# Splitting the value products of a tiled attention kernel by columns

## The chip, the cores and the metric

The kernel runs on one core of a Trainium2 chip. The metric is the device time of one execution in microseconds (us), as the median of several runs. Durations inside an execution come from one execution that was recorded by the hardware profiler.

TensorE is the engine that multiplies matrices (its rows are named PE in the profile, and PEld for the loading of weights that goes before a product). ScalarE (ACT) computes activations, VectorE (DVE) computes elementwise operations and reductions, GpSimd (POOL) does elementwise work on on-chip memory and issues DMAs, and SyncE (SP) issues DMAs. TensorE writes its results into eight accumulator banks of 128 partitions by 512 float32 columns, called `bank` here.

## What is computed

For x of 2048 tokens by 448, the reference mixes a 16-head attention block and an MLP by a gate for each token:

```python
def reference(A_x, A_wqkv, A_wo, B_x, B_w1, B_b1, B_w2, B_b2, gate_w):
    x = A_x
    g = _sigmoid((x * gate_w).sum(-1, keepdims=True))
    a = _A_ref(x, A_wqkv, A_wo)
    b = _B_ref(x, B_w1, B_b1, B_w2, B_b2)
    return g * a + (1 - g) * b
...
    scores = jnp.einsum("bhqd,bhkd->bhqk", q, k) * (Dh ** -0.5)
    p = _softmax(scores, axis=-1)
    o = jnp.einsum("bhqk,bhkd->bhqd", p, v)
```

`_A_ref` is attention with heads of 28 columns and a projection by wo, `_B_ref` is layer norm, a product by w1, GELU, and a product by w2. All data are float32.

## The kernel before

The kernel has three stages. The first one computes queries, keys, values and the gate (lines 125 to 260). The second one is the MLP (lines 435 to 499). The third one is the attention (lines 611 to 715), and the change lies in it.

The 16 heads are treated as 4 groups of 4 heads, and the 2048 queries as 4 chunks of 512 (`CH`). A group and a chunk together give 16 combinations, and the code numbers them `n`; I call each of them a chunk from here on. For each chunk the keys come in 16 steps of 128 (`NT`). One key tile of one head is a unit, so that there are 64 units to a chunk and 1024 in all. The outer loop takes five units at a time (`U`); such a turn crosses steps and chunks freely, there are 205 turns, and a chunk lasts 12.8 of them.

A turn consists of these parts, in the order in which TensorE gets them:

- `scores` (line 620) makes the score tiles of the first three units in banks 0 to 2. Each tile is the sum of three products of 28 or 29 rows by 512 columns (line 629), since keys and queries are held as a high and a low part. ScalarE then takes the exponential of the three banks in one instruction (line 634) into a tile `pt`. The other two units follow in banks 3 and 4, with a second exponential. Products of different heads use different groups of 32 rows of the array.
- In between up to three tiles of the row maximum of a later chunk are made in banks 5, 6 and 5 (`filler.max.issue`, line 321). VectorE reduces each of them (line 301). `filler.due` deals them out evenly over the turns until the maxima of all chunks are there.
- The value products `pv_mm` (line 655) multiply the exponentials by the values, and sum over the 16 steps of a chunk in bank 7. One step is four products, one for each head, of 128 rows by 512 columns; each writes 32 partitions of the bank, so that the four run beside each other in four groups of 32 columns of the array. The operands are float32, and the profile shows two records for each such product, with a weight load before each.

The order on TensorE is the program's order, as is that of the other engines in this loop (`tc.manual_schedule`). The lines that the change touches are 655 to 659 and 698 to 714: after the scores of a turn, all steps whose units had been made by the end of the turn before are summed, in whole steps, and not beyond the end of a chunk. Since a turn brings 1.25 steps, three turns of four sum one step and the fourth sums two.

When a chunk's sum is complete, `finish` (line 535) begins: VectorE copies bank 7 to `ob` (line 540), and GpSimd starts a DMA that gathers the denominators (line 541). The later parts of `finish` follow a fixed number of turns behind (`STEPS`): a reciprocal (line 543), DMAs that spread it (lines 545 and 547), three operations on GpSimd (lines 553 to 555), and in the last group also the projection by wo (lines 525 to 527). The next chunk's first value product has to wait for the copy. After the last turn the remaining steps are summed and `finish_last` (line 565) projects the last chunk and writes it out. There the sums over the denominators are made with four products of 128 by 128 in float32 (line 578).

The tiles `pt` come from a pool with four buffers for the three-unit form and four for the two-unit form.

Of the kernel before, what the change touches and what calls it, by code (L numbers as in the profile page):

```python
# [15 lines left out]
P = 128  # L16
# [5 lines left out]
NG = 4  # L22
CH = 512
NC = S // CH
NT = S // P
# [7 lines left out]
MG = 6  # L33
FS = 4
LQ = 12
STEPS = (2, 5, 7, 8, 9, 10)


@with_exitstack
def kernel(ctx: ExitStack, tc: tile.TileContext, xt, wqk, wv, wo, xk, w1, b1, w2, b2,  # L40
                          ident_d, sel_d, out):
    nc = tc.nc
# [344 lines left out]
    def load_khi(g):  # L387
        if g == MLP_G:
            khi[g] = khr
        else:  # L390
            khi[g] = aq.tile([P, S], F32R, name=f"khi{g}")
            for j in range(4):
                r = D + (4 * g + j) * DH
                nc.sync.dma_start(khi[g][32 * j:32 * j + DH].bitcast(F32), qk[0, r:r + DH])
        nc.sync.dma_start(khi[g][DH:P:32].bitcast(F32),
                          ones.rearrange("(a b) x -> a (b x)", a=1).partition_broadcast(4).rearrange("a o x -> a (o x)"))
# [3 lines left out]
    def load_klo(g):  # L400
        klo[g] = aq.tile([P, S], F32R, name="klo", bufs=2)
        for j in range(4):
            r = D + (4 * g + j) * DH
            nc.sync.dma_start(klo[g][32 * j:32 * j + DH].bitcast(F32), qk[1, r:r + DH])

    vg = {}

    def load_v(g):
        vg[g] = aq.tile([P, NT, P], F32, name="vg", bufs=2)
        for t in (slice(0, 4), slice(4, NT)):  # L410
            nc.sync.dma_start(vg[g][:, t], vs[t, :, g, :].rearrange("t p d -> p t d"))
# [3 lines left out]
    def load_q(n):  # L415

        g, c = divmod(n, NC)
        qs[n] = aq.tile([P, CH], F32R, name="qh", bufs=3), aq.tile([P, CH], F32R, name="ql", bufs=3)
        for i in range(2):
            for j in range(4):  # L420
                r = (4 * g + j) * DH
                nc.sync.dma_start(qs[n][i][32 * j:32 * j + DH].bitcast(F32), qk[i, r:r + DH, c * CH:(c + 1) * CH])

    def load_qm(n):

        while filler.done < min(65 * NG * NC, 65 * (n + 1) + 9):
            filler.max.issue(5, 1)
        g, c = divmod(n, NC)
        nc.sync.dma_start(qs[n][0][DH:P:32].bitcast(F32), ms[g][:, c * CH:(c + 1) * CH])
# [76 lines left out]
    U, UA = 5, 3  # L506
# [83 lines left out]
    def load_wo(g):  # L590
        worw = ao.tile([P, D], F32, name="ob")
        nc.sync.dma_start(worw, wo[:, g])
        nc.vector.tensor_copy(woh[:, g], worw)
        nc.gpsimd.tensor_sub(wol[:, g], worw, woh[:, g].bitcast(F32))

    def load_acc(c):

        a = aq.tile([P, NT, P], F32, name="vg", bufs=2) if c % 2 == 0 else aq.tile([P, S], F32, name="klo", bufs=2)
        if c % 2 == 0:
            a = a.rearrange("p a b -> p (a b)")  # L600
        acc[c] = a[:, :TPC * D].rearrange("p (t d) -> p t d", d=D)
        nc.sync.dma_start(acc[c], gbs[c * TPC:(c + 1) * TPC].rearrange("t p d -> p t d"))

    def gate_acc(c):
        for i in range(TPC):
            a, tt = acc[c][:, i], c * TPC + i
            nc.gpsimd.tensor_add(a, a, b2b)
            nc.gpsimd.tensor_scalar(a, a, ngate[:, tt:tt + 1], None, op0=OP.mult)
# [6 lines left out]

    filler.spread(nc.gpsimd, NG * NC * 65, ((NG * NC - 2) * NT + LQ - 1) * 4 // U)

    probs = {}

    def scores(units, most):  # L620

        def product(u, i):
            n, k, j = u // 4 // NT, u // 4 % NT, u % 4
            g, (qh, ql) = n // NC, qs[n]
            a, b, r = ((khi[g], qh, DH + 1), (klo[g], qh, DH), (khi[g], ql, DH))[i]
            r = slice(32 * j, 32 * j + r)
            nc.tensor.matmul(bank[:, u % U], a[r, k * P:(k + 1) * P], b[r], start=(i == 0), stop=(i == 2))  # L629

        def exps(units):
            t = ap.tile([P, len(units), CH], F32, name=f"pt{len(units)}")
            b = units[0] % U
            nc.scalar.activation(t, bank[:, b:b + len(units)], AF.Exp, scale=SCALE)  # L634
            for i, u in enumerate(units):
                probs[u] = t[:, i]

        first, last = units[:UA], units[UA:]
        if most > 0:
            filler.max.issue(5, 1, [(first[0] + 3) % 4])  # L640
        for i in range(3):
            for u in first:
                product(u, i)
        exps(first)
        for i in range(3):
            for u in last:
                product(u, i)
            if i == 0 and most > 1:
                filler.max.issue(6, 1, [(first[0] + 1) % 4, (first[0] + 2) % 4])
        if last:  # L650
            exps(last)
        if most > 2:
            filler.max.issue(5, 1, [(first[0] + 1) % 4, (first[0] + 2) % 4])

    def pv_mm(step):
        n, k = divmod(step, NT)
        for j in range(4):
            nc.tensor.matmul(pv[32 * j:32 * j + 32, :], vg[n // NC][:, k, 32 * j:32 * j + 32], probs.pop(4 * step + j),  # L658
                             start=(k == 0), stop=(k == NT - 1), skip_group_check=True)

    pv = bank[:, 7]
    E = mybir.EngineType
    steps = NG * NC * NT
    with tc.manual_schedule(engines={E.SP, E.Pool, E.Activation, E.DVE}):
        fin = None
        summed = 0
        ready = 0
        at = -1
        since = 0
        for u in range(0, 4 * steps, U):  # L670
            units = list(range(u, min(u + U, 4 * steps)))
            while at < units[-1] // 4:
                at += 1
                n, k = divmod(at, NT)
                g, c = divmod(n, NC)
                if n == 0:
                    if k == 0:
                        load_khi(1)
                        nc.sync.dma_start(b2b, b2.partition_broadcast(P))
                    if 2 <= k < 6:  # L680
                        load_wo(k - 2)
                    if k in (8, 10):
                        load_khi(k // 2 - 2)
                if g == NG - 1:
                    if k == 6:
                        load_acc(c)
                    if k == 10:
                        gate_acc(c)
                if k == 2 and n + 1 < NG * NC:
                    load_q(n + 1)  # L690
                if k == LQ and n + 1 < NG * NC:
                    load_qm(n + 1)
                if g + 1 < NG:
                    if c == 1 and k == 4:
                        load_klo(g + 1)
                    if c == 2 and k == 4:
                        load_v(g + 1)
            scores(units, min(3, filler.due()))
            ended = False
            while summed < ready and not ended:  # L700
                pv_mm(summed)
                summed += 1
                ended = summed % NT == 0
            ready = (units[-1] + 1) // 4
            since += 1
            if ended:
                n = summed // NT - 1
                fin, since = finish(n // NC, n % NC, pv), 0
                next(fin)
            elif fin is not None and since in STEPS:  # L710
                next(fin, None)
        while summed < steps:
            pv_mm(summed)
            summed += 1
        finish_last(NC - 1, pv)


# [51 lines left out]
```

## Time and profile before

| | |
|---|---|
| three runs | 1142.76, 1151.25, 1155.83 us; median 1151.25 us |
| the profiled execution | 1146.98 us, of which the span from the first to the last instruction is 1145.2 us |
| granted TensorE clock, mean over the span | 0.991 |
| attention, first turn to the last value products | about 486 to 1131 us of the span |
| TensorE busy between 500 and 1000 us | over 99.8% in each stretch of 100 us |
| ScalarE busy in the same stretches | 79 to 81% |
| VectorE busy in the same stretches | 68 to 69% |

Times of single instructions are read from the timeline, whose rows give the start in us from the beginning of the span, the duration (for a merged row, from the first start to the last end), the engine, the line, the operation, output and input, shapes and the count. In brackets stands how long the engine had been idle before, and what ended the idle time. Rows of TensorE's products overlap, since products are pipelined and their ends are modelled; the distance between starts is what a sequence costs.

### The profile page before, as it was taken

What the parts mean: (1) busy time and instruction counts of PE and PEld (TensorE: products, weight loads), DVE (VectorE), ACT (ScalarE), POOL (GpSimd) and SP (SyncE); (2) the same over time, 40 slices, a digit from 0 to 9 for tenths busy, and PEclk for the clock granted to TensorE, in tenths of its full rate; (3) what the DMA queues carried; (4) which work ended last, traced back from release to release, by engine and by line L of the source; (5) the groups of instructions that cost most, each with busy time, mean ns of one, the idle gap of its engine ahead of it and who ended that gap; (6) DMA issues with size and microseconds to landing.
All of it is one profiled execution on the core that took longest, in us unless ns stands there. A gap on an engine that the chain in (4) does not pass through costs nothing.

```text
span 1145.2 us, 19823 instructions
## 1 busy us (share of the span) xinstructions
PE 1116.6 (98%) x8136; PEld 678.4 (59%) x8136; DVE 731.6 (64%) x1033; ACT 635.9 (56%) x668; POOL 331.0 (29%) x355
## 2 busy tenths in 40 slices
PE   6999989999999999989999999999999999999998
PEld 4778867777767777744444444444444444454556
DVE  3433287888878888666676766676676667646103
ACT  5324551132033032067887878878787887848463
POOL 4043367146044032011123012311222123444250
PEclk9999999999999999989999999999999999999999
DMA  8878643002100014062101211111121003002201
GB/s 269 277 217 303 208 141 88 25 9 68 47 23 18 25 30 114 25 168 72 30 12 36 52 40 40 36 27 39 31 64 36 18 19 91 12 25 68 66 26 49
DMA packets 53519, 84.35 MB, mean 74 GB/s; under 512 B 8676, under 2 KB 28660, under 8 KB 52628
## 3 DMA queue, kind: packets, MB, share of 16 engines
q1 hardware_dynamic: 49236, 76.96, 22.5%
q0 software_dynamic: 4192, 6.12, 2.1%
q8 instruction: 64, 1.05, 0.4%
q14 instruction: 27, 0.22, 0.1%
HBM read 56.40 MB, written 26.49 MB: 72 GB/s over the span
## 4 chain that ended last, share of the span: by engine, by line
PE 89%; DMA 4%; POOL 3%; DVE 2%; issue 1%; ACT 1%; SPq 0%; POOLq 0%; ACTq 0%; DVEq 0%
PE bank L658 22%; PE bank L629 20%; PE bank L321 15%; PE bank L451 10%; PE bank L168 4%; PE bank L466 4%; PE bank L463 4%; PE bank L464 4%; PE bank L184 2%; PE bank L525 1%; DMA bxr<-in_xk 1%; PE bank L526 1%; PE bank L527 1%; DMA xraw<-in_xt 1%; POOL hl L456 1%
## 5 line engine op out<-in xcount | busy, mean ns | idle before, releaser
L634 ACT ACTIVATE pt<-bank 128x1536 f32<-128x1536 f32 (+1 forms) x410 | 484.6, 1234 | 155.9 <-PE bank L629 155.9
L301 DVE TENSOR_REDUCE mx<-bank 128x1 f32<-128x512 f32 x624 | 413.4, 687 | 174.9 <-PE bank L321 161.0
L658 PE MATMUL bank<-pt,vg 128*32 128x512 f32 x2048 | 263.7, 606 | 0.0
L303 DVE TENSOR_REDUCE mx<-bank 128x2 f32<-128x1024 f32 x200 | 235.4, 1219 | 41.1 <-PE bank L321 41.0
L321 PE MATMUL bank<-khi,qd 28*128 28x512 f32 x512 | 241.6, 479 | 0.3 <-DVE mx L301 0.2
L321 PEld LDWEIGHTS bank<-khi,qd 28*128 28x128 f32 x512 | 92.3, 181 | 148.3 <-DVE mx L301 107.0
L629 PE MATMUL bank<-qh,klo 28*128 28x512 f32 x1024 | 179.0, 395 | 0.0
L629 PE MATMUL bank<-qh,khi 29*128 29x512 f32 x768 | 161.8, 484 | 0.3 <-ACT h L469 0.3
L451 PE MATMUL bank<-y,w1f 128*128 128x512 f32 x616 | 153.2, 400 | 0.6 <-ACT h L455 0.6
L451 PEld LDWEIGHTS bank<-y,w1f 128*128 128x128 f32 x616 | 113.8, 190 | 36.1 <-issue 12.5
L629 PE MATMUL bank<-ql,khi 28*128 28x512 f32 x768 | 133.6, 393 | 0.0
L456 POOL TENSOR_TENSOR hl<-h,hh 128x512 fp32r<-128x512 f32 x56 | 72.5, 1295 | 172.0 <-ACT h L455 160.8
L658 PEld LDWEIGHTS bank<-pt,vg 128*32 128x32 f32 x2048 | 45.7, 108 | 84.6 <-issue 83.1
L629 PEld LDWEIGHTS bank<-qh,klo 28*128 28x128 f32 x1024 | 90.2, 186 | 4.2
L321 PE MATMUL bank<-khr,qd 28*128 28x512 f32 x512 | 80.7, 467 | 7.3 <-DVE mx L303 4.2
L541 POOL DMA_DIRECT2D lt<-ob x15 | 10.8, 723 | 265.7 <-DVE ob L540 265.7
L466 PE MATMUL bank<-w2h,hl 128*128 128x448 f32 x224 | 85.1, 380 | 1.9 <-POOL hl L456 1.9
L469 ACT ACTIVATE h<-bank 128x448 f32<-128x448 f32 x16 | 8.7, 543 | 140.4 <-PE bank L466 140.4
L629 PEld LDWEIGHTS bank<-qh,khi 29*128 29x128 f32 x768 | 63.3, 183 | 36.8 <-ACT pt L634 32.1
L463 PE MATMUL bank<-w2h,hh 128*128 128x448 f32 x224 | 84.7, 378 | 0.3 <-ACT hh L454 0.3
L454 ACT ACTIVATE hh<-bank,b1s 128x512 fp32r<-128x512 f32 x56 | 38.4, 685 | 81.9 <-PE bank L451 81.8
L464 PE MATMUL bank<-w2l,hh 128*128 128x448 f32 x224 | 82.3, 368 | 0.0
(100 smaller groups left out, 1237.0 us busy)
## 6 DMA issues: line engine op xcount, KB each, us to landing
qk<-hl SPq DMA_DIRECT2D x28, 512.0 KB
xraw<-in_xt SPq DMA_DIRECT2D x16, 256.0 KB
vs<-vt SPq DMA_DIRECT2D x16, 256.0 KB
r<-in_xt SPq DMA_DIRECT2D x16, 256.0 KB
rc<-rls POOLq DMA_DIRECT2D x60, 64.0 KB, 2.2
bxr<-in_xk SPq DMA_DIRECT2D x8, 448.0 KB
r<-in_w SPq DMA_DIRECT2D x14, 256.0 KB
gbs<-h SPq DMA_DIRECT2D x16, 224.0 KB
```

Of the source, the lines that this page charges most:

```text
L168: nc.tensor.matmul(ps, a, b, start=(i == 0), stop=(i == len(ops) - 1))
L301: nc.vector.reduce_max(self.mx[:, c0:c0 + 1], bank[:, b0], axis=AX)
L303: nc.vector.reduce_max(self.mx[:, c0:c1 + 1:c1 - c0], bank[:, b0:b1 + 1], axis=AX)
L321: nc.tensor.matmul(bank[:, b], self.qds[self.n][r, i * P:(i + 1) * P], khi[self.n // NC][r, k * 512:(k + 1) * 512], start=True, stop=True)
L451: nc.tensor.matmul(ps, a, b, start=(i == 0), stop=(i == len(ops) - 1))
L456: nc.gpsimd.tensor_sub(hl[f], h, hh[f].bitcast(F32))
L463: nc.tensor.matmul(a, hh[f][:, sl], w2h[f], start=(f == 0), stop=False)
L464: nc.tensor.matmul(a, hh[f][:, sl], w2l[f], start=False, stop=False)
L466: nc.tensor.matmul(a, hl[f][:, sl], w2h[f], start=False, stop=(f == NF - 1))
L629: nc.tensor.matmul(bank[:, u % U], a[r, k * P:(k + 1) * P], b[r], start=(i == 0), stop=(i == 2))
L634: nc.scalar.activation(t, bank[:, b:b + len(units)], AF.Exp, scale=SCALE)
L658: nc.tensor.matmul(pv[32 * j:32 * j + 32, :], vg[n // NC][:, k, 32 * j:32 * j + 32], probs.pop(4 * step + j), start=(k == 0), stop=(k == N ...
```

## The change

The value products are no longer issued in whole steps. `pv_mm` gets a number of columns up to which all has to be summed (512 to a step), and cuts a step where that number falls into it. `share` computes this number for a turn: within a chunk it rises linearly with the turn, from 0.6 turns (`LAG`) after the chunk's first turn to the turn in which its last units are summed, rounded down to a multiple of 128 columns, and never beyond the units that were made by the end of the turn before. In the turn with which a chunk ends, all that is left of it is summed.

```diff
+LAG = 0.6
...
-    def pv_mm(step):
-        n, k = divmod(step, NT)
-        for j in range(4):
-            nc.tensor.matmul(pv[32 * j:32 * j + 32, :], vg[n // NC][:, k, 32 * j:32 * j + 32], probs.pop(4 * step + j),
-                             start=(k == 0), stop=(k == NT - 1), skip_group_check=True)
+    def pv_mm(upto):
+
+        nonlocal summed
+        while summed < upto:
+            step, a = divmod(summed, CH)
+            b = min(CH, a + upto - summed)
+            n, k = divmod(step, NT)
+            for j in range(4):
+                nc.tensor.matmul(pv[32 * j:32 * j + 32, a:b], vg[n // NC][:, k, 32 * j:32 * j + 32],
+                                 probs[4 * step + j][:, a:b], start=(k == 0), stop=(k == NT - 1), skip_group_check=True)
+            summed += b - a
+
+    def share(turn):
+
+
+        ready = turn * U // 4
+        n = min(NG * NC - 1, summed // (NT * CH))
+        first, last = (-(-NT * 4 * i // U) for i in (n, n + 1))
+        part = (turn - first - LAG) / (last - first - LAG)
+        return min(ready, steps, (n + 1) * NT) * CH if part >= 1 else min(ready * CH, n * NT * CH + int(NT * CH * part) // P * P)
...
             scores(units, min(3, filler.due()))
-            ended = False
-            while summed < ready and not ended:
-                pv_mm(summed)
-                summed += 1
-                ended = summed % NT == 0
-            ready = (units[-1] + 1) // 4
+            before = summed // (NT * CH)
+            pv_mm(share(u // U))
+            ended = summed // (NT * CH) > before
             since += 1
             if ended:
-                n = summed // NT - 1
+                n = before
...
-        while summed < steps:
-            pv_mm(summed)
-            summed += 1
+        pv_mm(steps * CH)
```

More of the change, by code (lines that the diff above doesn't have):

```diff
@@ L653, in scores @@
             filler.max.issue(5, 1, [(first[0] + 1) % 4, (first[0] + 2) % 4])
-    def pv_mm(step):
-        n, k = divmod(step, NT)
-        for j in range(4):
-            nc.tensor.matmul(pv[32 * j:32 * j + 32, :], vg[n // NC][:, k, 32 * j:32 * j + 32], probs.pop(4 * step + j),
-                             start=(k == 0), stop=(k == NT - 1), skip_group_check=True)
+    def pv_mm(upto):
[14 more added lines that the diff above has]
+        return min(ready, steps, (n + 1) * NT) * CH if part >= 1 else min(ready * CH, n * NT * CH + int(NT * CH * part) // P * P)
     pv = bank[:, 7]
+    summed = 0
     E = mybir.EngineType
@@ L665 @@
         fin = None
-        summed = 0
-        ready = 0
         at = -1
```

## The prediction, made before the changed kernel was run

> **What bounds the kernel now.** I read the engines' busy time first, then the chain that ended last, then the waits, then the timeline of some turns.
>
> ```profile
> PE 1116.6 (98%) x8136; PEld 678.4 (59%) x8136; DVE 731.6 (64%) x1033; ACT 635.9 (56%) x668; POOL 331.0 (29%) x355
> ...
> PE 89%; DMA 4%; POOL 3%; DVE 2%; issue 1%; ACT 1%; SPq 0%; POOLq 0%; ACTq 0%; DVEq 0%
> PE bank L658 22%; PE bank L629 20%; PE bank L321 15%; PE bank L451 10%; PE bank L168 4%; PE bank L466 4%; PE bank L463 4%; PE bank L464 4%; PE bank L184 2%; PE bank L525 1%; DMA bxr<-in_xk 1%; PE bank L526 1%; PE bank L527 1%; DMA xraw<-in_xt 1%; POOL hl L456 1%
> ```
>
> TensorE is on the chain for 89%, and the three lines of an attention turn (value products 658, scores 629, row maxima 321) hold 57% of the span. A busy TensorE may still hide small waits, and evening out the turns could only win if there are such waits. The table of waits has one that fits:
>
> ```profile
> PEld bank L629 <- ACT pt L634: 40.4, 133, 0.8
> ```
>
> In 133 cases a score's weight load waited for an exponential. Whether this costs time shows in two turns that follow each other, the first of them behind one step of value products (8 records), the second behind two (16):
>
> ```profile
> 704.08 1.07 PE L658 MATMUL bank<-pt,vg 128*32 128x512 f32 x8
> ...
> 705.07 0.18 PEld L321 LDWEIGHTS bank<-khi,qd 28*128 28x128 f32 x1 [0.84 <-DVE mx L301]
> ...
> 705.87 0.18 PEld L629 LDWEIGHTS bank<-qh,khr 29*128 29x128 f32 x2 [0.25 <-ACT pt L634]
> ...
> 706.15 2.37 ACT L634 ACTIVATE pt<-bank 128x1536 f32<-128x1536 f32 x2 [0.34 <-PE bank L629]
> ...
> 706.78 0.16 PEld L658 LDWEIGHTS bank<-pt,vg 128*32 128x32 f32 x8 [0.25 <-issue]
> 706.78 1.92 PE L658 MATMUL bank<-pt,vg 128*32 128x512 f32 x16
> ...
> 708.63 0.18 PEld L321 LDWEIGHTS bank<-khi,qd 28*128 28x128 f32 x1 [0.84 <-issue]
> ...
> 709.72 2.37 ACT L634 ACTIVATE pt<-bank 128x1536 f32<-128x1536 f32 x2 [1.20 <-PE bank L629]
> ...
> 710.34 1.06 PE L658 MATMUL bank<-pt,vg 128*32 128x512 f32 x8
> ...
> 711.33 0.18 PEld L321 LDWEIGHTS bank<-khi,qd 28*128 28x128 f32 x1 [0.84 <-DVE mx L301]
> ```
>
> A turn begins with the weight load of line 321 (705.07, 708.63, 711.33). From there to its value products it takes 706.78 - 705.07 = 1.71 us in the turn that waits 0.25 us for ScalarE, and 710.34 - 708.63 = 1.71 us in the turn behind the double portion, where ScalarE had been idle for 1.20 us and nothing waits for it. So the wait lies beside other work: five units on four row groups mean that one group has six products in a row, and these take the 1.71 us. ScalarE is just in time: its two exponentials end at 706.15 + 2.37 = 708.52, that is 3.45 us after the turn's start. Both kinds of turn are bound by TensorE, with 1.71 us of scores each.
>
> **The change part by part.** One step costs from start to start 705.07 - 704.08 = 0.99 us, two steps 708.63 - 706.78 = 1.85 us. So 512 columns stream in 0.86 us, and 0.13 us are fixed for each turn. A turn of 640 columns then takes 1.25 x 0.86 + 0.13 = 1.21 us. Four turns before: 4 x 1.71 + 3 x 0.99 + 1.85 = 11.66 us. Four after: 4 x (1.71 + 1.21) = 11.68 us. The evening out by itself is worth nothing: columns are moved between turns that TensorE bounds alike.
>
> *Pieces.* Working `share` through for all turns gives 402 pieces in place of 256 whole steps: 110 of 512 columns, 88 of 384, 116 of 256, 88 of 128. That is 146 pieces and 292 passes more (a float32 product runs in two passes; each has four records and four weight loads). No value product under 512 columns is in the trace. The nearest rows are the float32 products of 128 columns behind the last turn, and the weight loads of the value products:
>
> ```profile
> 1132.57 1.05 PE L578 MATMUL bank<-ob,sel 128*128 128x128 f32 x8
> ```
> ```profile
> L578 PE MATMUL bank<-ob,sel x8: 270/275/275, 1132.6 to 1133.3; 128*128 128x128 f32 x8
> ```
> ```profile
> L658 PEld LDWEIGHTS bank<-pt,vg x2048: 106/109/153, 494.2 to 1129.7; 128*32 128x32 f32 x187
> ```
> ```profile
> 707.24 0.13 PEld L658 LDWEIGHTS bank<-pt,vg 128*32 128x32 f32 x4 [0.30 <-issue]
> ```
>
> Eight passes of 128 columns start (1.05 - 0.275) / 7 = 0.111 us apart, although each loads new weights. A quarter of a 512-column pass is 0.86 / 2 / 4 = 0.107 us. So a pass costs about 0.004 us beyond its columns: 292 x 0.004 = 1.2 us. From below the bound is nothing, since all columns are still streamed. From above, every extra pass would pay a whole weight load of 0.109 us: 292 x 0.109 = 31.8 us. In between, a set of four loads takes 0.13 us, which is longer than a 128-column pass by 0.023 us: 176 such passes x 0.023 = 4.0 us. I take 1.2 us, because line 578 is the same type and the same width. The Trainium skill, page "TensorEngine Tiling (Array Packing)", section "Instruction Overhead", speaks against short pieces: it gives each matmul some 60 cycles of overhead, at 2.4 GHz about 0.025 us, an estimate by which the pieces would cost 292 x 0.025 = 7.3 us and the whole change 11 us; the row of line 578 does not show such an overhead.
>
> *The first turn of a chunk.* With `LAG`, a chunk's first value products are 256 columns instead of 512, in the turn behind the one that ended a chunk. There the copy of bank 7 comes before the reductions on VectorE:
>
> ```profile
> 723.06 0.18 PEld L321 LDWEIGHTS bank<-khi,qd 28*128 28x128 f32 x1 [0.84 <-DVE mx L301]
> ...
> 723.27 0.69 DVE L540 COPY ob<-bank 128x512 f32<-128x512 f32 x1 [0.37 <-PE bank L658]
> ...
> 723.88 1.96 DVE L301 TENSOR_REDUCE mx<-bank 128x1 f32<-128x512 f32 x3
> ...
> 724.13 2.37 ACT L634 ACTIVATE pt<-bank 128x1536 f32<-128x1536 f32 x2 [0.28 <-PE bank L629]
> ...
> 724.61 0.18 PEld L321 LDWEIGHTS bank<-khi,qd 28*128 28x128 f32 x1 [0.17 <-DVE mx L301]
> ...
> 725.04 1.06 PE L658 MATMUL bank<-pt,vg 128*32 128x512 f32 x8
> ...
> 726.03 0.18 PEld L321 LDWEIGHTS bank<-khi,qd 28*128 28x128 f32 x1 [0.84 <-DVE mx L301]
> ```
>
> VectorE is done with the third reduction at 723.88 + 1.96 = 725.84. The next turn's first product needs the same bank 5 and begins at 726.03; it doesn't wait. With 256 columns it could begin at 725.04 + 0.99 - 0.43 = 725.60, but waits until 725.84 and about 0.04 us more (the load at 724.61 stands 0.04 us behind the first reduction, 723.88 + 0.69): 725.88, a loss of 0.28 us. All of the turn's scores are queued behind this load on TensorE. The 256 columns that were put off cost their 0.43 us later. ScalarE ends at 724.13 + 2.37 = 726.50, before the second group of the next turn wants its banks (725.88 + 0.80, as 705.87 stands to 705.07), so it adds nothing. Of the 15 chunk ends before the last, 14 lie among turns with row maxima: 14 x 0.28 = 3.9 us. Bounds: nothing, if the copy begins earlier; 0.43 us for each, 6.0 us, if VectorE is late by more.
>
> *Turns without row maxima*, about eight behind 1081 us, are the exception in which ScalarE does bind:
>
> ```profile
> 1084.77 0.21 PEld L629 LDWEIGHTS bank<-qh,khi 29*128 29x128 f32 x4 [0.84 <-ACT pt L634]
> ...
> 1086.37 1.07 PE L658 MATMUL bank<-pt,vg 128*32 128x512 f32 x8
> ...
> 1087.37 0.19 PEld L629 LDWEIGHTS bank<-qh,khi 29*128 29x128 f32 x3 [0.84 <-ACT pt L634]
> 1088.27 0.18 PEld L629 LDWEIGHTS bank<-qh,khi 29*128 29x128 f32 x2 [0.37 <-ACT pt L634]
> ...
> 1089.17 1.06 PE L658 MATMUL bank<-pt,vg 128*32 128x512 f32 x8
> ```
>
> Behind two steps the scores take 1086.37 - 1084.77 = 1.60 us, behind one step 1089.17 - 1087.37 = 1.80 us. Evened out, two turns form a loop: exponentials end 3.45 us after a start, 0.05 us later the next turn's second group begins, 0.90 us later (1089.17 - 1088.27) its value products, then 1.21 us: 5.61 / 2 = 2.81 us a turn. Four turns before were 2 x 1.60 + 2 x 1.80 + 3 x 0.99 + 1.85 = 11.62, after 11.24 us: 0.8 us won over eight turns. The first turn of the last chunk has 256 columns there too; the turn behind it then reaches its value products 3.45 + 0.05 + 0.90 = 4.40 us after that start instead of 1.60 + 0.56 + 1.80 = 3.96: 0.4 us back. I count nothing.
>
> *What does not move.* The instructions of ScalarE, VectorE, GpSimd and SyncE stay in the same order, and every chunk ends in the same turn as before, so `finish` and its DMAs keep their turns. The sums lag the units by at most 1.75 steps, under two turns; with four buffers of `pt` no exponential waits for one. The tail behind the last turn gets 768 columns instead of 512, and turn 204 has 256 fewer: nothing.
>
> The sum: 1.2 + 3.9 = +5.1 us. Against the profiled execution (1146.98 us: span 1145.2 and 1.8 around it) that gives 1152.1 us. That execution lies 4.3 us under the median of the three runs, 1151.25 us, by which it would be 1156.4. I forecast 1154 us, between the two.
>
> **The rivals.** *Slower: TensorE isn't supplied with instructions fast enough.*
>
> ```profile
> 700.00:800.00 100.00, 100.00 (x958) 47.30 (x951) 68.81 (x109) 80.86 (x69) 17.61 (x26) 1.00 0.10 26
> ```
>
> TensorE got 958 products (each with its weight load) in 100 us, one in 0.104 us, and the turn of 26 pairs (15 scores, 3 maxima, 8) in 2.70 us and that of 34 in 3.56 us have the same rate. The changed kernel has on average 18 + 402 x 8 / 204 = 33.8 pairs in a turn of 2.92 us, one in 0.086 us. If pairs can't come faster than 0.104 us, a turn takes 3.52 us, and some 190 turns lose 0.6 us each: +114 us, about 1265 us. It decides from 0.086 us a pair upwards; at 0.089 us it costs 17 us. Against it: value passes start exactly as far apart as their columns need, and at 706.78 eight weight loads go within 0.16 us, so a stock of instructions lay ready. The skill's page "TensorE: Matmul & The Clock Gate", section "Wait — 56ns, not 53.3ns?", puts the sequencer at about 62 ns for each MATMUL, by which the average turn would be supplied and this rival would fall; no run here shows that number. Chance 0.20, about half of it within 20 us.
>
> *Faster: the waits for ScalarE cost time after all.* In an even turn the exponentials end 3.45 us after its start, that is 0.53 us into the next turn, 0.27 us before they are needed. If all 40.4 us of the wait's row are on the path, the kernel comes to 1147 + 5 - 40 = 1112 us. For it speaks the loss of 0.20 us in the turns without maxima; against it the two equal 1.71 us. Chance 0.08.
>
> *Hidden: the 0.28 us at chunk ends don't appear*, since VectorE's copy starts earlier or some other turn gives it back. Then +1.2 us at most, 1148 to 1152 us. Chance 0.12.
>
> **How the numbers follow.** My forecast has 0.60; with its unknown terms at their upper ends (4.0 and 6.0) it gives +10 us, and 0.06 of the chance I put beyond 1%, as for a price of weight loads nearer to its upper bound. One per cent, 11.5 us, is about what runs that spread from 1142.8 to 1155.8 can tell from no change. Slower by over 1%: 0.20 + 0.06 = 0.26; faster: 0.08; within: 0.66. The range reaches down to 1144, the lowest run with 1.2 us for the pieces, and up to 1172, the median with 17 us of the slower rival and the pieces' 4 us; it leaves out the faster rival and half of the slower one.
>
> **What would show it.** Right: 9304 records of products instead of 8136; 1.71 us from a turn's start to its value products in nearly all turns; 1.21 us for a 640-column turn; 128-column passes 0.11 us apart; the wait of line 629 for ScalarE much shorter than 40.4 us without a gain; and behind each chunk end a load of line 321 that waits for VectorE about 0.3 us after the value products. Wrong: scores in 1.5 us or less behind even turns, value passes of 128 columns 0.13 us or more apart, or gaps put down to issue.

## The result, and the profile after

| | before | changed |
|---|---|---|
| median of 20 runs each | 1148.3 us | 1153.66 us |
| lowest and highest | 1141.6 to 1155.83 us | 1148.78 to 1157.96 us |
| ratio changed / before, 95% interval | | 1.0047 (1.0032 to 1.0061) |
| the profiled execution | 1146.98 us, span 1145.2 us | 1154.30 us, span 1152.5 us |

The changed kernel is slower by 0.47%, or 5.4 us, which is within one per cent, with the whole interval above 1. In the changed kernel the lines are numbered differently from line 36 on: the scores are line 630, the row maxima 322, the value products 664, the exponentials 635, the copy 541.

The page of the changed kernel begins with the busy time of the engines; the second and third line quoted are the chain that ended last:

```profile
PE 1122.8 (97%) x9304; PEld 741.6 (64%) x9304; DVE 733.4 (64%) x1033; ACT 636.4 (55%) x668; POOL 331.0 (29%) x355
...
PE 86%; DVE 4%; DMA 4%; POOL 3%; issue 2%; ACT 1%; SPq 0%; DVEq 0%; POOLq 0%; ACTq 0%
PE bank L664 21%; PE bank L630 19%; PE bank L322 13%; PE bank L452 10%; PE bank L169 5%; PE bank L467 4%; PE bank L464 4%; PE bank L465 4%; PE bank L185 3%; DVE mx L302 2%; PE bank L526 1%; DMA bxr<-in_xk 1%; PE bank L527 1%; PE bank L528 1%; DMA lt<-ob 1%
```

There are 9304 products, 1168 more than before, as the 402 pieces ask for. VectorE has 4% of the chain instead of 2%: its reductions (line 302) now stand in it. In the table of waits the wait of the scores for the exponentials has shrunk from 40.4 us to this, while the kernel got slower:

```profile
PEld bank L630 <- ACT pt L635: 9.3, 21, 0.8
```

Two even turns from the timeline of the changed kernel:

```profile
704.37 1.28 PE L664 MATMUL bank<-pt,vg 128*32 128x256 f32 x16
...
705.58 0.18 PEld L322 LDWEIGHTS bank<-khi,qd 28*128 28x128 f32 x1 [0.62 <-DVE mx L302]
...
706.67 2.37 ACT L635 ACTIVATE pt<-bank 128x1536 f32<-128x1536 f32 x2 [0.55 <-PE bank L630]
...
707.29 1.28 PE L664 MATMUL bank<-pt,vg 128*32 128x128 f32 x16
...
708.50 0.18 PEld L322 LDWEIGHTS bank<-khi,qd 28*128 28x128 f32 x1 [0.84 <-DVE mx L302]
```

From value products to the next turn it is 705.58 - 704.37 = 1.21 us, and from there to the value products 707.29 - 705.58 = 1.71 us. ScalarE is idle for 0.55 us ahead of this turn's exponentials, and the scores take 1.71 us as they did when they waited for it. (A merged row shows the shape of its first product; the two portions are 256 and 384 columns, and 128 and 512.)

Behind a chunk's end, in the turn with 256 columns:

```profile
726.51 0.18 PEld L322 LDWEIGHTS bank<-khi,qd 28*128 28x128 f32 x1 [0.84 <-DVE mx L302]
...
726.72 0.69 DVE L541 COPY ob<-bank 128x512 f32<-128x512 f32 x1 [0.81 <-PE bank L664]
...
727.33 1.96 DVE L302 TENSOR_REDUCE mx<-bank 128x1 f32<-128x512 f32 x3
...
728.06 0.18 PEld L322 LDWEIGHTS bank<-khi,qd 28*128 28x128 f32 x1 [0.32 <-DVE mx L302]
...
728.49 0.64 PE L664 MATMUL bank<-pt,vg 128*32 128x256 f32 x8
...
729.34 0.18 PEld L322 LDWEIGHTS bank<-khi,qd 28*128 28x128 f32 x1 [0.69 <-DVE mx L302]
```

The next turn begins 729.34 - 728.49 = 0.85 us behind the value products, where 256 columns need 0.43 + 0.13 = 0.56 us. The third reduction ends at 727.33 + 1.96 = 729.29, and the load follows 0.05 us later. This is the stall that was forecast, with 0.29 us. It stands behind 13 of the 14 chunk ends in question. At the fourteenth the turn has only two row maxima to reduce, and nothing stalls, with the same 256 columns and the same copy ahead of the reductions:

```profile
996.00 1.28 DVE L302 TENSOR_REDUCE mx<-bank 128x1 f32<-128x512 f32 x2
...
996.99 0.64 PE L664 MATMUL bank<-pt,vg 128*32 128x256 f32 x8
...
997.56 0.18 PEld L322 LDWEIGHTS bank<-khi,qd 28*128 28x128 f32 x1 [0.41 <-DVE mt L291]
```

It is 997.56 - 996.99 = 0.57 us.

Where the whole difference went can be counted in the timelines. The spans differ by 7.3 us. Of these 1.9 us lie ahead of the sixth turn of the attention (it begins at 507.62 us before and 509.49 us after), and 5.4 us between it and the last turn:

```profile
507.62 0.18 PEld L321 LDWEIGHTS bank<-khr,qd 28*128 28x128 f32 x1 [0.84 <-DVE mx L301]
...
1126.11 0.19 PEld L629 LDWEIGHTS bank<-qh,khi 29*128 29x128 f32 x3 [0.84 <-ACT pt L634]
```
```profile
509.49 0.18 PEld L322 LDWEIGHTS bank<-khr,qd 28*128 28x128 f32 x1 [0.20 <-issue]
...
1133.42 0.19 PEld L630 LDWEIGHTS bank<-qh,khi 29*128 29x128 f32 x3 [0.84 <-ACT pt L635]
```

In the changed kernel the last turn begins at 1133.42 us: 1133.42 - 509.49 = 623.9 us against 1126.11 - 507.62 = 618.5 us. I took the times from turn start to value products and back from the rows of all turns in between. Fitted over the undisturbed turns, value products cost 0.138 us for a turn, 0.853 us for 512 columns, and 0.005 us for a piece. By this fit, and beyond it:

| part | before | changed |
|---|---|---|
| stalls behind the first 256 columns of a chunk, 13 of 14 places | - | 3.9 us |
| the last chunk's start, where ScalarE is late (as worked out ahead) | - | 0.4 us |
| 146 pieces at 0.005 us | - | 0.7 us |
| two turns in which the reciprocal waits for its DMA, 0.85 and 1.05 us | - | 1.9 us |
| 384 columns more in this stretch, at 0.853 us for 512 | - | 0.6 us |
| other small waits, in sum, that are gone in the changed kernel | 2.1 us | - |

That sums to 3.9 + 0.4 + 0.7 + 1.9 + 0.6 - 2.1 = +5.4 us. The fifth row is no cost of the change: the kernel before sums 2560 columns in the turns ahead of this stretch and the changed kernel 2176, and both end with the same number. The change itself costs 4.8 us here. The second, the fourth and the last row were not in the prediction's sum. The first of the two late turns, with the reciprocal in VectorE's queue ahead of the reductions, and the same reciprocal in the kernel before:

```profile
809.02 0.18 PEld L322 LDWEIGHTS bank<-khi,qd 28*128 28x128 f32 x1 [0.62 <-DVE mx L302]
...
810.31 0.25 DVE L544 RECIPROCAL lt<-lt 128x16 f32<-128x16 f32 x1 [1.66 <-DMA lt<-ob]
810.48 1.90 DVE L302 TENSOR_REDUCE mx<-bank 128x1 f32<-128x512 f32 x3
...
811.16 0.18 PEld L322 LDWEIGHTS bank<-khi,qd 28*128 28x128 f32 x1 [0.90 <-DVE mx L302]
...
811.58 0.38 PEld L664 LDWEIGHTS bank<-pt,vg 128*32 128x32 f32 x16 [0.24 <-issue]
```
```profile
806.27 0.25 DVE L543 RECIPROCAL lt<-lt 128x16 f32<-128x16 f32 x1 [0.50 <-DMA lt<-ob]
```

The gathered denominators land late, VectorE stands for 1.66 us, the third row maximum waits for the first reduction, and the scores take 811.58 - 809.02 = 2.56 us. Two things come together there. The time from issue to landing of this small DMA (line 541, then 542) varies a lot between chunks, first before, then changed:

```profile
DMA to landing us min/median/max: 2.1/2.9/5.6
```
```profile
DMA to landing us min/median/max: 2.1/2.3/6.0
```

At these two places it is long in both kernels: 5.6 and 5.0 us before, 5.7 and 6.0 us changed. And the two turns from the copy to the turn with the reciprocal lasted 6.54 us before at both places, since one of the two had a double portion; in the changed kernel they last 5.73 and 5.74 us.

The 1.9 us at the start go with the granted clock. The columns of this view are a stretch, its length, busy time and instructions of PE, PEld, DVE, ACT and POOL, the granted clock, the DMA share and GB/s; first before, then changed:

```profile
480.00:510.00 30.00, 26.74 (x188) 15.14 (x186) 13.62 (x25) 15.05 (x14) 4.53 (x4) 0.83 0.52 132
```
```profile
480.00:510.00 30.00, 27.18 (x186) 16.70 (x187) 11.88 (x22) 13.63 (x13) 4.54 (x4) 0.72 0.54 134
```

The granted clock is 0.83 in one and 0.72 in the other. It is 0.50 from 493 to 502 us before, and from 492 to 506 us in the changed kernel. It is not a property of the change: the third experiment below, whose portions are those of the kernel before, also shows 0.72, and the fifth, whose portions are those of the changed kernel, shows 0.83.

### The profile page after: what moved, and what is told of

Same layout as the page of the kernel before. It is cut to its first block, busy times and chain, and to the rows that moved or that the text cites. A ratio compares the mean times of both kernels' runs of the same rounds, so it can differ in the third digit from the quotient of the medians.

```text
span 1152.5 us, 22159 instructions
## 1 busy us (share of the span) xinstructions
PE 1122.8 (97%) x9304; PEld 741.6 (64%) x9304; DVE 733.4 (64%) x1033; ACT 636.4 (55%) x668; POOL 331.0 (29%) x355
## 4 chain that ended last, share of the span: by engine, by line
PE 86%; DVE 4%; DMA 4%; POOL 3%; issue 2%; ACT 1%; SPq 0%; DVEq 0%; POOLq 0%; ACTq 0%
PE bank L664 21%; PE bank L630 19%; PE bank L322 13%; PE bank L452 10%; PE bank L169 5%; PE bank L467 4%; PE bank L464 4%; PE bank L465 4%; PE bank L185 3%; DVE mx L302 2%; PE bank L526 1%; DMA bxr<-in_xk 1%; PE bank L527 1%; PE bank L528 1%; DMA lt<-ob 1%
## 5 line engine op out<-in xcount | busy, mean ns | idle before, releaser
L664 PE MATMUL bank<-pt,vg 128*32 128x256 f32 (+3 forms) x3216 | 265.4, 447 | 0.0
L322 PE MATMUL bank<-khi,qd 28*128 28x512 f32 x512 | 234.6, 462 | 4.1 <-DVE mx L302 4.1
L630 PE MATMUL bank<-qh,klo 28*128 28x512 f32 x1024 | 194.8, 397 | 0.0
L630 PE MATMUL bank<-qh,khi 29*128 29x512 f32 x768 | 174.3, 480 | 0.6 <-ACT pt L635 0.3
L664 PEld LDWEIGHTS bank<-pt,vg 128*32 128x32 f32 x3216 | 81.9, 109 | 108.5 <-issue 98.0
L630 PE MATMUL bank<-ql,khi 28*128 28x512 f32 x768 | 145.4, 394 | 0.0
L630 PEld LDWEIGHTS bank<-qh,klo 28*128 28x128 f32 x1024 | 102.9, 188 | 1.6
L630 PEld LDWEIGHTS bank<-ql,khi 28*128 28x128 f32 x768 | 77.8, 188 | 9.3
```

What stands on the lines that cost most here:

```text
L322: nc.tensor.matmul(bank[:, b], self.qds[self.n][r, i * P:(i + 1) * P], khi[self.n // NC][r, k * 512:(k + 1) * 512], start=True, stop=True)
L664: nc.tensor.matmul(pv[32 * j:32 * j + 32, a:b], vg[n // NC][:, k, 32 * j:32 * j + 32], probs[4 * step + j][:, a:b], start=(k == 0), stop=( ...
```

## The experiments

Each was timed in five rounds beside the kernel before. All are edits of the changed kernel, but for the last one.

| experiment | ratio to the kernel before, 95% interval | sixth to last turn |
|---|---|---|
| the changed kernel | 1.0047 (1.0032 to 1.0061) | 623.9 us |
| 1: LAG = 0 | 0.9989 (0.9968 to 1.001) | 619.0 us |
| 2: whole steps, half a step first | 1.0029 (1.0009 to 1.005) | 624.3 us |
| 3: whole steps in quarters | 1.0031 (1.0008 to 1.0055) | 622.2 us |
| 4: whole steps in eighths | 1.0384 (1.0346 to 1.0421) | 656.8 us |
| 5: copy on ScalarE | 1.0023 (1.0006 to 1.0041) | 622.0 us |
| 6: STEPS from 3 | 1.0013 (0.9996 to 1.0031) | 622.1 us |
| 7: LAG = 0, copy on ScalarE | 0.9952 (0.993 to 0.9975) | 615.0 us |
| 8: the same, STEPS from 3 | 0.9954 (0.9932 to 0.9977) | 614.2 us |
| 9: the kernel before, copy on ScalarE | 0.9976 (0.9956 to 0.9995) | 616.0 us |
| (the kernel before) | 1 | 618.5 us |

The last column is worked out from the turn starts of one profiled execution each, as above; the clock at the start of the attention doesn't touch it, but for experiment 4. Inside this part the granted clock fell in experiment 2 (0.66 from 1089 to 1094 us, where two turns lose 1.6 us) and in experiment 4 (0.91 from 540 to 560 us).

**1: even portions without the short first turn.**

```diff
-LAG = 0.6
+LAG = 0.0
```

> The changed kernel with LAG = 0: the portions are still even and cut into pieces (355 pieces, 99 more than whole steps), but the first turn of a chunk gets 512 columns instead of 256. My theory (a stall of 0.28 us behind each of 14 chunk ends, 0.005 us for each extra piece, nothing for the evening out): the stalls go, 99 x 0.005 = 0.5 us stay, the ratio to the kernel before is 1.000 to 1.001, and from a chunk's first value products to the next turn it takes 0.99 us. Rival A (the pieces carry all of the 5.4 us, 0.037 us for each of 146): 99 x 0.037 = +3.7 us, ratio 1.003. Rival B (even turns win by the waits for ScalarE, and the chunk ends hid it): ratio under 0.999.

Measured: 1146.84 us against 1147.66 us, ratio 0.9989. The turns behind a chunk's end have 512 columns and begin their successors without a stall:

```profile
729.06 0.69 DVE L541 COPY ob<-bank 128x512 f32<-128x512 f32 x1 [0.59 <-PE bank L664]
...
730.83 1.07 PE L664 MATMUL bank<-pt,vg 128*32 128x512 f32 x8
...
731.83 0.18 PEld L322 LDWEIGHTS bank<-khi,qd 28*128 28x128 f32 x1 [0.84 <-DVE mx L302]
```

It is 731.83 - 730.83 = 1.00 us. The portions are 640 columns in 114 of the 205 turns (134 in the changed kernel), and the ratio is 1 within its interval: evening out by itself moves nothing that these runs can tell. Rival A's 1.003 lies above the interval. Rival B's "under 0.999" isn't excluded by the interval. In the trace the stretch of turns takes 619.0 us, 0.5 us more than before, but one turn loses 1.2 us there, as the denominators land late (its scores take 698.23 - 695.34 = 2.89 us). So a gain of the size of the 40.4 us of waits is excluded, and one of about 1 us is not.

**2: the short first turn alone.**

```diff
-        return min(ready, steps, (n + 1) * NT) * CH if part >= 1 else min(ready * CH, n * NT * CH + int(NT * CH * part) // P * P)
+        upto = min(ready, steps, (n + 1) * NT) * CH
+        return min(upto, summed + CH // 2) if n and summed == n * NT * CH else upto
...
-                                 probs[4 * step + j][:, a:b], start=(k == 0), stop=(k == NT - 1), skip_group_check=True)
+                                 probs[4 * step + j][:, a:b], start=(k == 0 and a == 0), stop=(k == NT - 1), skip_group_check=True)
```

> The portions of the kernel before, in whole steps, but in the first turn of each chunk behind the first one only half a step (256 columns), the other half in the next turn: 15 extra pieces, nothing evened out. My theory: 14 stalls of 0.28 us, some 0.4 us in the one chunk start without row maxima, 15 x 0.005 us for the pieces: +4.4 us, ratio 1.003 to 1.005, nearly all that the change cost. Rival A (the pieces carry it): 15 x 0.037 = 0.6 us, ratio 1.0005.

(In the second edit the flag that begins a sum is set for the first piece of a chunk alone.)

Measured: 1150.06 us, ratio 1.0029, just under the 1.003 to 1.005 that was expected, which lies inside its interval. With fifteen extra pieces and a short first turn, most of what the change costs is there. The stall is the same as in the changed kernel:

```profile
723.07 0.64 PE L664 MATMUL bank<-pt,vg 128*32 128x256 f32 x8
723.92 0.18 PEld L322 LDWEIGHTS bank<-khi,qd 28*128 28x128 f32 x1 [0.70 <-DVE mx L302]
```

Again 0.85 us instead of 0.56. Rival A (1.0005) lies below the interval.

**3 and 4: many pieces, portions as before.**

```diff
-            b = min(CH, a + upto - summed)
+            b = min(CH, a + upto - summed, a + P)
...
-        return min(ready, steps, (n + 1) * NT) * CH if part >= 1 else min(ready * CH, n * NT * CH + int(NT * CH * part) // P * P)
+        return min(ready, steps, (n + 1) * NT) * CH
```

(`P // 2` in place of `P` for the eighths; the starting flag as in experiment 2.)

> The portions of the kernel before, but every step cut into four pieces of 128 columns: 1024 pieces, 768 more than before, and 58 instead of 28 pairs of load and product in an average turn. My theory (0.005 us for each extra piece, from the fit of the changed kernel's turns): +3.8 us, ratio 1.003 to 1.004, two steps still 1.85 to 1.90 us from start to start. Rival A (the pieces carry the change's 5.4 us, 0.037 us each): +28 us, ratio 1.025. The slower rival of the prediction (a pair of load and product can't come faster than one in 0.104 us): turns of 6 us in place of 2.9, over +500 us; it shows from 0.05 us a pair upwards.

> As before, but every step cut into eight pieces of 64 columns: 2048 pieces, 1792 more, a pass of 0.053 us with four weight loads each, and 98 pairs in an average turn of 2.92 us, one in 0.030 us. My theory carried on (0.005 us for each extra piece): +9 us, ratio 1.008. If a set of four weight loads (0.13 us in a row of the trace before) can't be hidden behind shorter passes: 4096 passes x (0.13 - 0.053) = +315 us, ratio 1.27; that would be a floor which the changed kernel's 128-column pieces don't reach yet.

Measured: quarters 1150.31 us, ratio 1.0031, where 1.003 to 1.004 was expected for 0.005 us a piece; the stretch of turns is 622.2 - 618.5 = 3.7 us longer. In the timeline of the quarters a single step and a double one:

```profile
705.35 1.08 PE L664 MATMUL bank<-pt,vg 128*32 128x128 f32 x32
706.36 0.18 PEld L322 LDWEIGHTS bank<-khi,qd 28*128 28x128 f32 x1 [0.20 <-DVE mx L302]
...
708.08 1.95 PE L664 MATMUL bank<-pt,vg 128*32 128x128 f32 x64
709.96 0.18 PEld L322 LDWEIGHTS bank<-khi,qd 28*128 28x128 f32 x1 [0.20 <-issue]
```

They take 1.01 and 1.88 us, against 0.99 and 1.85 before: 0.02 to 0.03 us for three or six more pieces. The scores' 1.71 us stay too (708.08 - 706.36 = 1.72), although a turn holds twice as many pairs of load and product. So the slower rival of the prediction, a supply of one pair in 0.104 us, is refuted down to about 0.05 us.

The eighths cost more: 1191.17 us, ratio 1.0384, where the price of a piece would have given 1.008 and a set of loads that can't be hidden 1.27. Neither was right. An undisturbed portion still runs as fast as its columns:

```profile
669.78 0.94 PEld L664 LDWEIGHTS bank<-pt,vg 128*32 128x32 f32 x64 [0.25 <-issue]
...
669.78 1.10 PE L664 MATMUL bank<-pt,vg 128*32 128x64 f32 x64
```

Sixty-four products take 1.10 us from the first start to the last end, where thirty-two of 128 columns took 1.08. But in some turns the products break off, and nothing that the profile shows was waited for:

```profile
665.11 0.64 PE L664 MATMUL bank<-pt,vg 128*32 128x64 f32 x28
...
667.39 0.59 PEld L664 LDWEIGHTS bank<-pt,vg 128*32 128x32 f32 x36 [1.81 <-issue]
667.39 0.75 PE L664 MATMUL bank<-pt,vg 128*32 128x64 f32 x36 [1.65 <-issue]
```

One portion of 64 is cut in two by 1.65 us. The table of waits counts 12 such breaks, 15.1 us in all, the longest of 4.8 us:

```profile
PE bank L664 <- issue: 15.1, 12, 4.8
```

That fits a lack of instructions, at 98 pairs in a turn; that it is one, and what would supply them too late, was not tried. The breaks are less than half of the 656.8 - 618.5 = 38.3 us that the turns became longer. The price of a piece would make some 9 us of the rest; where the others go was not followed up.

**5: is it the copy or the short turn that stalls?**

```diff
-        nc.vector.tensor_copy(ob, pv)
+        nc.scalar.activation(ob, pv, AF.Copy)
```

> The changed kernel (LAG = 0.6) with the copy of bank 7 to ob on ScalarE instead of VectorE. The question is whether the stall behind a chunk's first 256 columns comes from the copy ahead of the reductions. Theory C (the copy is the cause, as the prediction put it): both the wait of the third maximum in that turn (0.27 us) and the stall behind it (0.29 us) go at 14 chunk ends, -7.8 us against the changed kernel, ratio to the kernel before 0.998. Theory T (the short turn is the cause: a turn's third reduction ends some 2.6 us after the turn's start with or without the copy, and a turn with 256 columns lasts 2.28 us): only the 0.27 us go, the 0.29 us stay, -3.8 us against the changed kernel, ratio 1.001. If ScalarE is late by the copy, more than 1.0047.

Measured: 1150.11 us, ratio 1.0023; theory T had 1.001, theory C 0.998, and the interval excludes C. The trace decides it:

```profile
721.96 0.18 PEld L322 LDWEIGHTS bank<-khi,qd 28*128 28x128 f32 x1 [0.84 <-DVE mx L302]
722.22 0.61 ACT L541 ACTIVATE ob<-bank 128x512 f32<-128x512 f32 x1
722.50 2.00 DVE L302 TENSOR_REDUCE mx<-bank 128x1 f32<-128x512 f32 x3 [1.12 <-PE bank L322]
...
723.67 0.64 PE L664 MATMUL bank<-pt,vg 128*32 128x256 f32 x8
724.55 0.18 PEld L322 LDWEIGHTS bank<-khi,qd 28*128 28x128 f32 x1 [0.72 <-DVE mx L302]
```

The copy runs on ScalarE, and the scores of this turn take 723.67 - 721.96 = 1.71 us instead of 1.98 (728.49 - 726.51). The stall behind it stays: 724.55 - 723.67 = 0.88 us. The third reduction ends at 722.50 + 2.00 = 724.50, 2.54 us after the turn's start, and a turn of 256 columns would be over after 1.71 + 0.56 = 2.27 us. Three row maxima a turn need turns of about 2.6 us even without the copy, and of 729.34 - 726.51 = 2.83 us with it. The stretch of turns is 1.9 us shorter than the changed kernel's, half of what theory T had: in the next turn a score's load waits for ScalarE, which is late by the copy, and this turn takes 0.1 us more (727.57 - 724.55 = 3.02 us, against 708.50 - 705.58 = 2.92).

**6: the reciprocal one turn later.**

```diff
-STEPS = (2, 5, 7, 8, 9, 10)
+STEPS = (3, 5, 7, 8, 9, 10)
```

> The changed kernel with STEPS beginning at 3 instead of 2: the reciprocal of the denominators, which sits in VectorE's queue ahead of the reductions and waits for a DMA, comes one turn later. In the changed kernel's profile two turns lost 0.85 and 1.05 us there. If that is part of what the change cost: the two losses go and the ratio to the kernel before is 1.003 instead of 1.0047. If the landing was late in that execution by chance: ratio as before, 1.0045 to 1.005.

Measured: 1149.32 us, ratio 1.0013, below the 1.003 that was expected, with 1.003 inside the interval. In the trace the two late turns are gone, and the stretch of turns is 623.9 - 622.1 = 1.8 us shorter, as those two had cost 1.9 us. They were hardly there by chance alone: in the trace of experiment 5 the same two turns take 0.27 and 1.20 us more than 2.92 us.

**7 and 8: what the runs suggest.** The first has these edits, the second the one of experiment 6 as well:

```diff
-LAG = 0.6
+LAG = 0.0
...
-        nc.vector.tensor_copy(ob, pv)
+        nc.scalar.activation(ob, pv, AF.Copy)
...
-                                 probs[4 * step + j][:, a:b], start=(k == 0), stop=(k == NT - 1), skip_group_check=True)
+                                 probs[4 * step + j][:, a:b], start=(k == 0 and a == 0), stop=(k == NT - 1), skip_group_check=True)
```

> LAG = 0, the copy of bank 7 on ScalarE, and the flag that begins a sum set for the first piece of a chunk alone. No stall behind chunk ends and no wait of the third maximum: 14 x 0.27 = 3.8 us under the version with LAG = 0 alone, ratio to the kernel before 0.995 to 0.997. If ScalarE pays for the copy what VectorE saves (its exponentials are late by 0.6 us in that turn): ratio 1.000.

> As the version with LAG = 0 and the copy on ScalarE, with STEPS beginning at 3 too: if late landings cost 1 to 2 us in an execution, ratio 0.994 to 0.996; if they cost nothing on average, the same as without.

Measured: 1142.33 us (0.9952) and 1140.35 us (0.9954) against 1147.04 us for the kernel before, both as expected. Both beat the two kernels of this study. The later reciprocal can't be told from none by the ratios.

**9: does that need the even portions?** The kernel before with the edit of experiment 5.

> The kernel before with one edit, the copy of bank 7 on ScalarE: does the gain of the version with LAG = 0 need the even turns at all? If not, 14 x 0.27 = 3.8 us are won here too, ratio 0.996 to 0.997. If it does: behind a turn of one step (2.71 us) ScalarE's exponentials end 3.45 - 2.71 = 0.74 us into the next turn, the copy of about 0.6 us follows, the exponentials that are due at 1.08 us begin at 1.34 us, and the turn after that waits about 0.25 us for ScalarE: nothing won where a chunk ends with one step, ratio 0.999 to 1.001.

Measured: 1144.58 us against 1148.1 us, ratio 0.9976. It lies between the two forecasts, and the interval reaches into both; the trace decides. There the 13 turns behind chunk ends that have three row maxima are each shorter by 0.20 to 0.29 us, 3.3 us together, and one turn with late denominators takes 0.6 us back. The gain is there without even turns, and the reason against it fell: the copy does come ahead of the exponentials, but delays them by little.

```profile
722.43 0.18 PEld L321 LDWEIGHTS bank<-khi,qd 28*128 28x128 f32 x1 [0.84 <-DVE mx L301]
723.11 0.60 ACT L540 ACTIVATE ob<-bank 128x512 f32<-128x512 f32 x1
...
723.59 2.39 ACT L634 ACTIVATE pt<-bank 128x1536 f32<-128x1536 f32 x2
...
724.18 0.16 PEld L658 LDWEIGHTS bank<-pt,vg 128*32 128x32 f32 x8 [0.28 <-issue]
```

The exponential begins 723.59 - 722.43 = 1.16 us after the turn's start instead of 1.08 us, since it follows the copy's start by 0.48 us, not by its whole 0.60 us, and the copy itself began 0.06 us earlier than worked out. What the even portions of experiment 7 add to it, 0.9952 against 0.9976, lies within the two intervals; the stretch of turns is 1.0 us shorter.

## Why the prediction was right, and where not

*The bound.* TensorE bounds a turn, and the waits for ScalarE lay beside other work. Shown by the wait that fell from 40.4 to 9.3 us without a gain, and by experiment 1, to within the 1 to 2 us of small waits that went.

*Evening out is worth nothing.* 1.21 us for 640 columns and 1.71 us for the scores, both as worked out; the interval of experiment 1 includes 1. The trace of the changed kernel has 2.1 us of small waits less than the one before, which the prediction did not foresee.

*Pieces.* Forecast 1.2 us, measured 0.7 us (146 x 0.005), confirmed by the quarters at five times as many pieces. The choice of the row of line 578, between bounds of nothing and 31.8 us, was the step that carried most of the risk. The rule of the Trainium skill that was weighed there ("TensorEngine Tiling (Array Packing)", section "Instruction Overhead", some 60 cycles for each matmul, 0.025 us) would have given 768 x 2 x 0.025 = 38 us for the quarters, read as a cost that is added to each product. They cost 0.31%, 3.6 us of 1148, so this reading is refuted here.

*The first turn of a chunk.* Forecast 3.9 us, found 3.9 us in the trace, and the short first turn alone gives a ratio of 1.0029. But the step that named the copy on VectorE as the cause failed: the prediction put the stall down to the copy that "comes before the reductions", and experiment 5 shows it without the copy, while the one short turn with two row maxima has the copy and no stall. The cause is that a turn of 256 columns is shorter than the time that a turn's three reductions take after its start. The number came out right, though the cause was wrong, because the copy delays the value products of that turn (by 0.27 us) as much as the reductions (0.24 us).

*Turns without row maxima.* Counted as nothing. The 0.4 us of the last chunk's first turn appeared; of the 0.8 us to be won, 0.3 us did.

*What does not move.* This step was incomplete. The order of all queues stayed, but at two chunk ends the turns up to the reciprocal became 0.8 us shorter, and with them the time that the DMA has. Together with landings that took 0.15 and 1.0 us longer than before, this cost 1.9 us. It was made up for by 2.1 us of small waits that went, which the prediction had not counted either. That the two omissions cancelled was luck.

*The time itself.* 1154 us stood on 1154 - 5.1 = 1148.9 us for the kernel before, a place chosen between one execution and the median of three runs. The median of 20 runs is 1148.3 us. That the measured 1153.66 us lies so close owes something to luck in this choice.

*The rivals.* The supply of instructions is refuted for 128-column pieces by experiment 3: at 58 pairs in a turn of 2.92 us one came every 0.050 us. (The 62 ns that the prediction weighed here, from the Trainium skill, "TensorE: Matmul & The Clock Gate", section "Wait — 56ns, not 53.3ns?", hold by that section only with hardware decode off; as a floor for a pair they are not borne out by this run.) Experiment 4 suggests that there is such a limit, between 58 and 98 pairs in a turn. The faster rival, with all of the 40.4 us, is refuted by experiment 1 and the row of waits, and the hidden one by the stall in the timeline.

## What to carry to other kernels

A wait that ends just in time costs nothing: before evening out such waits, compare a turn that has the wait with one that has not, from the start of its own work to the start of the next. When work is moved between turns, check the shortest turn that results against every engine that has a fixed amount of work in each turn, here three reductions; one short turn at each chunk's start cost more than all the cutting. Work that delays the bounding engine on a busy queue (the copy on VectorE) is better put on an engine that has time at that moment, and here this paid more than the scheduling did. A wait for a small DMA in the queue of an engine that others depend on needs room for its longest landing (here 6.0 us) and not for the median (2.3 us).

## What the runs showed of the hardware that was not expected

Float32 products of 128 rows by 32 columns, four side by side, run in pieces of 128 columns at a cost of 0.005 us a piece; 58 pairs of load and product went through an average turn of 2.9 us with no more loss than that, while 98 did not, with 12 breaks of up to 4.8 us for which the profile names no cause.

The gather of one chunk's denominators took between 2.1 and 6.0 us from issue to landing within one execution.

The granted clock between 480 and 510 us, where the attention begins, differed between executions: 0.72, 0.83 and, in experiment 7, 0.89, with TensorE busy for about 27 of the 30 us each time. Between the two kernels this went with a shift of 1.9 us, and it must be taken out before two traces are compared.
